# A derivative stored in the forward or recomputed in the backward: four layers of attention, forward and gradient, on one core

## The chip, the core and the metric

The kernel runs on one core of a Trainium2 chip. The core has five engines with their own instruction queues: PE (matrix products into PSUM, with weight loads beside them), DVE (elementwise and reductions), ACT (activations, copies), POOL (elementwise within SBUF) and SP (which here only issues transfers). ACT issues transfers too, from the same queue as its arithmetic. Every engine runs its queue in order. The metric is the time of one launch in microseconds; lower is better. "Granted clock" is the share of full speed that PE's clock had.

## The reference

Four layers over 2048 tokens of width 640, in 32 heads of 20, each with a normalisation in front and a residual around it: linear attention (A), sliding attention with a window of 256 (B), A, B. Both A layers share weights, as both B layers do.

```python
phi = lambda t: jnp.where(t > 0, t + 1, jnp.exp(t)) + 1e-6
pq, pk = phi(q), phi(k)
kv = jnp.einsum("bhsd,bhse->bhde", pk, v)
z = jnp.einsum("bhsd->bhd", pk)
num = jnp.einsum("bhqd,bhde->bhqe", pq, kv)
den = jnp.einsum("bhqd,bhd->bhq", pq, z)[..., None] + 1e-6
o = num / den
```

That is layer A, whose feature map is `phi`. Layer B is softmax attention. Outputs are the last x, the gradient for x and those for the four weight matrices; everything is bfloat16.

The derivative of `phi` is 1 for t > 0 and exp(t) otherwise, that is min(exp(t), 1). The kernel computes phi(t) as max(t, 1e-6) + min(exp(t), 1), so min(exp(t), 1) stands in a tile of its own on the way. From phi alone it can be had as min(phi - 1e-6, 1).

## The kernel before

Tokens are worked on in 16 tiles of 128. The layers are numbered 0 to 3 (A, B, A, B). The stages, with their places in the profiled span:

- First pass (up to about 120 us): for each tile normalise x (`ln`), multiply by layer 0's q, k and v weights, and apply `phi` (`a_qkv`, L488 to L538). Per half of 320 columns: PE into PSUM, ACT's exponential into a tile `ee` (L516), DVE's min with 1 in place (L517), DVE's max and add (L520) into `pp` (for q) or `gcar` (for k). `ee` is a ring of 4 buffers, `pp` one of 2. ACT copies part of v (L501). Results go to DRAM by transfers that ACT issues: `pq`, `pk`, `v`, and the two derivatives `eq` and `ek`.
- Token sums (`a_kv`): the products of pk and v, and pk's own sum, over all tokens. Three of five bands and the sum gather in the bank `pv_ps` (L597, L605) as the tiles come; these are fillers, which the order puts where PE has nothing else. The two other bands (`band_sum`, L579) take buffers of the ring `mm`, two PSUM banks that nearly all products share. DVE masks the sums into `mbd` and `zsel`.
- Joint passes, 0 and 2 (about 120 to 400 and 430 to 730 us; `ab_pass`): layers l and l+1 together, in a software pipeline over tiles. Steps of one tile are `num` (A's numerator and denominator, `a_num`, L448 and L646), `out` (A's projection, then layer l+1's normalisation), `qkv` (B's projections), the scores and weighted values of B's eight groups of heads (`attn`, L826, L830, L864), and `outb` (B's projection). Pass 0 has `a_first` for layer 2 behind that, k and v alone. Pass 2 has `late_q` for layer 2's q, and the first steps of the backward.
- Between the passes layer 2's sums are made; the first six tiles of its q (`EARLY`) are fillers there (`late_q`, matmuls L553, exponential L557); the weights are turned (L913), fillers too. The q of the first two tiles is turned by PE through a buffer of `mm` (L464), that of others by a transposing transfer on SP.
- Backward of layer 3 (about 740 to 1060 us), a stage for layers 3 and 2 (to 1460), backward of layer 1 (to 1770), a stage for layers 1 and 0 (to the end). In those two stages `lin_grads` (about 1220 to 1370, and 1940 to 2070 us) loads per tile pk, v and the numerator's gradient by transposing transfers, and the derivatives `eq` and `ek` by plain ones, all on SP. PE makes the gradients of phi(q) and phi(k) in PSUM, and DVE multiplies them by the derivative into `dqkv` (L1503). Beside it runs `tail`: PE's product with the weights, ACT's copy `dh` (L1309), DVE's `scr` (L1317), ACT's `w` (L1324), POOL's `gw` (L1327), DVE's update of `gcar` (L1329). In the stage for layers 3 and 2 also `local_dO`: PE's product, DVE's `slab` (L1370), POOL's `prod` (L1377), DVE's reduction (L1380) and two small ones (L1382, L1384), and a transfer `dOpt` that ACT issues.

Each engine's order in the forward and in the two stages is made ahead by a planner (`Sched.order`) from estimated costs: among the operations whose inputs it takes to be ready it picks the earliest start, then the place in the program (`prio`). Fillers are handicapped by 300 ns. A ring hands out its buffers in the program's order, so an operation that needs the ring's next buffer stands behind the one that is named earlier. In the forward PE's other operations may go at most `AHEAD` places past the first that isn't done. The program's order in a joint pass is sorted by positions: tile number plus an offset of each step, in the table `AT`, where 1.0 is one tile.

Of the kernel before, what the change touches and what calls it, by code (L numbers as in the profile page):

```python
# [20 lines left out]
LN_EPS = 1e-5  # L21
AHEAD = 19
IDLE = 300
# [179 lines left out]
class Kern:  # L203
    def __init__(self, ctx, tc, x0, A_wqkv, A_wo, B_wqkv, B_wo, grad_out, outs):
# [68 lines left out]
        for l in (0, 2):  # L273
            self.sv[l] = dict(
                pq=d.tile([T, D], BF, name=f"pq{l}"), pk=d.tile([T, D], BF, name=f"pk{l}"),
                eq=d.tile([T, D], BF, name=f"eq{l}"), ek=d.tile([T, D], BF, name=f"ek{l}"),
                v=d.tile([T, D], BF, name=f"v{l}"), o=d.tile([T, D], BF, name=f"o{l}"),
                r32=d.tile([T, self.H], F32, name=f"r32{l}"),
                mbd=d.tile([D, D + P], BF, name=f"mbd{l}"),
            )  # L280
# [53 lines left out]
    def forward(self, slabs):  # L334
# [5 lines left out]
        with ExitStack() as st:  # L340
# [72 lines left out]
            def dma(eng, out, in_, size, r, w, **kw):  # L413
                def f():
                    with nc.allow_non_contiguous_dma(reason="strided layouts"):
                        dq[eng].dma_start(out=out(), in_=in_())
                op(eng, 60, f, r, w, dma=("D", size), **kw)
# [70 lines left out]
            def a_qkv(l, tt, hnT):  # L488
# [3 lines left out]
                def chunk(ci):  # L492
                    def f():
# [29 lines left out]
                        if ci == 3 and "q" in c:  # L523
                            p_, e = c["p"], c["q"]
                            turn("s", lambda: pqT[:, :, tt * P:(tt + 1) * P], lambda: p_.t, DT, [(p_, 0), (p_, 1)],
                                 [("pqT", tt)])
                            dma("ACT", lambda: self.tm_view(sv["pq"])[:, tt, :], lambda: p_.t, 160 * KB,
                                [(p_, 0), (p_, 1)], [])
                            dma("ACT", lambda e=e: self.tm_view(sv["eq"])[:, tt, :], lambda e=e: e.t, 160 * KB,
                                [(e, 0), (e, 1)], [])  # L530
                        if ci == 3:
                            e = c["k"]
                            dma("ACT", lambda: self.tm_view(sv["pk"])[:, tt, :], lambda: pk[:, tt, :], 160 * KB,
                                [("pk", tt, 2), ("pk", tt, 3)], [])
                            dma("ACT", lambda e=e: self.tm_view(sv["ek"])[:, tt, :], lambda e=e: e.t, 160 * KB,
                                [(e, 2), (e, 3)], [])
                    return f
# [4 lines left out]
            def late_q(l, tt, where="s1", **F):  # L542
# [25 lines left out]
                dma("ACT", lambda: self.tm_view(sv["pq"])[:, tt, :], lambda: p_.t, 160 * KB, [(p_, 0), (p_, 1)], [], **F)  # L568
                dma("ACT", lambda: self.tm_view(sv["eq"])[:, tt, :], lambda: e.t, 160 * KB, [(e, 0), (e, 1)], [], **F)

# [392 lines left out]
            def a_first(items, l, base, lag=0.0, late=()):  # L963


                for tt in range(TT):
# [12 lines left out]

            EARLY = 6  # L980
            AT = {0: dict(num=-2.458, out=-1.707, outb=1.792, step=0.144, qkv=-0.99, wide=0.745, lag=0.42, af=2.042, al=-0.11),
                  2: dict(lq=-3.207, num=-2.403, out=-1.76, outb=1.696, step=0.086, qkv=-0.985, wide=0.584, lag=0.35, gT=0.745, dO=1.691, dOs=0.137)}

# [85 lines left out]
            a_kv(0)  # L1069
            ab_pass(0, False)  # L1070
            for tt in range(EARLY):
                late_q(2, tt, filler=True)
            a_kv(2)
            kv_users = {o for t in range(TT) for k in [("pk", t, 2), ("pk", t, 3), ("vv", t, 4), ("vv", t, 5)]
# [16 lines left out]
    def bwd_phase(self, lb, la, nb, ahead, raw):  # L1091
# [9 lines left out]
        with ExitStack() as st:  # L1101
# [363 lines left out]
            def lin_grads(tt, items, t0):  # L1465
# [4 lines left out]
                def start():  # L1470
                    for nm, src, size in (("dNT", self.tmp_dN, 192 * KB), ("pkT", sv["pk"], 160 * KB),
# [3 lines left out]
                             [("dNd", tt)] if nm == "dNT" else [], [b])  # L1475
                    c["eq"], c["ek"] = load("eq", sv["eq"], tt), load("ek", sv["ek"], tt)

# [415 lines left out]
```

## Time and profile before

| | |
|---|---|
| median of 3 runs | 2144.93 us (2142.76 to 2145.81) |
| the profiled execution | 2145.22 us, its span 2143.5 us |
| granted clock, mean | 0.975 |
| PE busy | 2008.2 us (94%) |
| DVE, ACT, POOL busy | 1440.1, 1203.3, 879.4 us |
| transfers | 376.43 MB, mean 176 GB/s |

The page names an instruction by its line and engine, then the tile written and those read. A time behind `<-` in brackets is what the engine idled before it and what ended the idling. `mm_ps`, `s_ps`, `pv_ps` and `dw_ps` are banks of PSUM. Tiles laid into the region `slabR` go by that name: there `slabR` can be the normalised rows, or in `lin_grads` the buffer of `ek`.

### The profile page before, as it was taken

How to read it: one execution, taken by the hardware profiler on the slowest of the kernel's cores; microseconds unless marked ns; L12 is line 12 of the kernel's file. 1: busy time of each engine (PE TensorE's matmuls, PEld its weight loads, DVE VectorE, ACT ScalarE, POOL GpSimd, SP SyncE). 2: the span in 40 equal slices, each digit the busy share in tenths (PEclk: the TensorE clock that was granted, in tenths of full speed). 3: DMA queues.
4: the chain of work that ended last, by engine and by line, in shares of the span. 5: the costliest groups of instructions: out<-in, count | busy, mean ns of one | idle time of the engine just before them, and what ended most of it. 6: DMA issues, size and time to landing. Idle time of an engine off the chain costs nothing. (4 is left out here: it accounts for less than half of the span.)

```text
span 2143.5 us, 68024 instructions
## 1 busy us (share of the span) xinstructions
PE 2008.2 (94%) x27908; PEld 1389.2 (65%) x27908; DVE 1440.1 (67%) x2954; ACT 1203.3 (56%) x1995; POOL 879.4 (41%) x1850
## 2 busy tenths in 40 slices
PE   6879999889999899999899999999999999999999
PEld 4656666656666577777666667656777765666764
DVE  6757777567776599999634368606998984444651
ACT  3527878647888589899422233216988881221430
POOL 1015666316777456666223223204665652230210
PEclk9989999999999899999899999999999999999999
DMA  9928989469998788987987899847999998989943
GB/s 291 256 106 179 191 193 191 119 198 201 210 208 191 146 157 151 161 161 155 193 185 168 213 200 203 175 104 142 157 158 151 170 170 162 199 185 227 186 111 102
DMA packets 943687, 376.43 MB, mean 176 GB/s; under 512 B 821776, under 2 KB 923664, under 8 KB 943120
## 3 DMA queue, kind: packets, MB, share of 16 engines
q1 hardware_dynamic: 866176, 299.16, 71.9%
q10 hardware_dynamic: 77200, 72.94, 11.1%
q8 instruction: 218, 3.57, 0.7%
q14 instruction: 93, 0.76, 0.1%
HBM read 109.02 MB, written 112.07 MB: 103 GB/s over the span
## 5 line engine op out<-in xcount | busy, mean ns | idle before, releaser
L1693 DVE TENSOR_TENSOR ds_sb<-pair,e_sb 128x768 bf16<-128x768 f32 x480 | 437.6, 951 | 57.8 <-PE pair L1654 49.6
L1673 ACT ACTIVATE e_sb<-pair 128x768 bf16<-128x768 f32 x480 | 390.9, 815 | 95.6 <-PE pair L1654 67.4
L839 POOL TENSOR_SCALAR_AFFINE_SELECT e_sb<-e_sb 128x384 bf16<-128x384 bf16 (+1 forms) x512 | 198.3, 406 | 357.5 <-ACT e_sb L830 335.7
L830 ACT ACTIVATE e_sb<-s_ps 128x1152 bf16<-128x1152 f32 (+2 forms) x256 | 273.8, 1070 | 100.2 <-PE s_ps L826 78.4
L1685 POOL TENSOR_SCALAR_AFFINE_SELECT e_sb<-e_sb 128x256 bf16<-128x256 bf16 x448 | 182.0, 406 | 227.1 <-ACT e_sb L1673 226.9
L1327 POOL TENSOR_TENSOR gw<-w,gcar 128x640 f32<-128x640 f32 x64 | 89.4, 1397 | 423.4 <-ACT w L1324 406.8
L1138 PEld LDWEIGHTS <-slabR 128*128 128x128 bf16 x1920 | 185.6, 98 | 116.1 <-DMA slabR<-o 3.7
L1682 POOL TENSOR_SCALAR_AFFINE_SELECT e_sb<-e_sb 128x256 bf16<-128x256 bf16 x512 | 206.5, 406 | 89.3 <-ACT e_sb L1673 89.3
L1718 PEld LDWEIGHTS <-dsT 128*128 128x128 bf16 x2880 | 146.2, 97 | 97.7 <-issue 91.5
L1709 ACT COPY dsT<-dsT_ps 128x768 bf16<-128x768 bf16 x240 | 191.2, 796 | 9.4 <-PE dsT_ps L1706 6.6
L448 PE MATMUL mm_ps<-slabR,hnTB 128*128 128x320 bf16 x960 | 170.5, 308 | 10.5 <-DVE gcar L520 6.0
L1706 PE MATMUL dsT_ps<-ident,ds_sb 128*128 128x128 bf16 x1848 | 158.2, 223 | 1.3 <-ACT dsT L1709 1.1
L1722 PEld LDWEIGHTS <-ds_sb 128*128 128x128 bf16 x2880 | 145.1, 96 | 0.8 <-issue 0.8
L1722 PEld LDWEIGHTS <-e_sb 128*128 128x128 bf16 x2880 | 145.0, 96 | 0.0
L844 POOL TENSOR_SCALAR_AFFINE_SELECT e_sb<-e_sb 128x512 bf16<-128x512 bf16 x224 | 142.6, 636 | 0.0
L833 ACT ACTIVATE e_sb<-s_ps 128x384 bf16<-128x384 f32 (+2 forms) x256 | 119.9, 468 | 32.3 <-PE s_ps L826 15.1
L1138 PE MATMUL dw_ps<-dqkv,slabR 128*128 128x480 bf16 x640 | 134.7, 366 | 0.0
L1309 ACT ACTIVATE dh<-mm_ps 128x320 f32<-128x320 f32 x64 | 28.0, 437 | 189.8 <-PE mm_ps L1138 164.9
L1138 PE MATMUL dw_ps<-dqkv,om 128*128 128x480 bf16 x640 | 134.2, 366 | 0.0
L1654 PE MATMUL pair<-slabR 32*128 32x384 bf16 (+2 forms) x1024 | 120.5, 326 | 12.0 <-DVE ds_sb L1693 5.2
L1138 PEld LDWEIGHTS <-om 128*128 128x128 bf16 x800 | 77.5, 98 | 71.3 <-DMA om<-o 2.4
L864 PEld LDWEIGHTS <-e_sb 128*128 128x128 bf16 x2880 | 105.5, 96 | 26.6 <-POOL e_sb L844 7.5
(234 smaller groups left out, 4357.6 us busy)
## 6 DMA issues: line engine op xcount, KB each, us to landing
qkvp<-qk_slab SPq DMA_DIRECT2D x64, 256.0 KB, 3.7
hn<-slabR SPq DMA_DIRECT2D x64, 160.0 KB, 2.9
qkvp<-v_slab SPq DMA_DIRECT2D x32, 256.0 KB, 3.4
slabR<-qkvp SPq DMA_DIRECT2D x16, 512.0 KB, 4.8
o<-o SPq DMA_DIRECT2D x48, 160.0 KB, 2.9
eq<-ee ACTq DMA_DIRECT2D x32, 160.0 KB, 3.0
pq<-pp ACTq DMA_DIRECT2D x32, 160.0 KB, 2.4
ek<-ee ACTq DMA_DIRECT2D x32, 160.0 KB, 2.7
```

Of the source, the lines that this page charges most:

```text
L448: nc.tensor.matmul(ps.t[:, w0:w0 + width], lhsT=lhsT(), rhs=rhs(), start=start, stop=stop)
L830: op("ACT", av(3 * nkt * P), lambda: nc.scalar.activation(e.t[:, 0:3, 0:nkt, :], s3.t[:, :, 0:nkt * P].rearrange("p h (i q) -> p h i q", q=P),
L839: nc.gpsimd.affine_select(out=v, in_=v, compare_op=ALU.is_ge, fill=0.0, base=0, pattern=[[0, h1 - h0], [1, P]], channel_multiplier=-1)
L1138: nc.tensor.matmul(ps.t[:, w0:w0 + width], lhsT=lhsT(), rhs=rhs(), start=start, stop=stop)
L1673: nc.scalar.activation(E[n][:, 2 * p:2 * p + 2], PR[h][:, :, 0:3 * P].rearrange("p i (j q) -> p i j q", q=P), ACT.Exp, scale=self.c_att)
L1682: nc.gpsimd.affine_select(out=e[:, :, j, :], in_=e[:, :, j, :], compare_op=ALU.is_ge, fill=0.0, base=0, pattern=[[0, 2], [-1, P]], channel ...
L1685: nc.gpsimd.affine_select(out=e[:, :, j, :], in_=e[:, :, j, :], compare_op=ALU.is_ge, fill=0.0, base=-1, pattern=[[0, 2], [1, P]], channel ...
L1693: nc.vector.tensor_mul(DS[n][:, hs], PR.pop(h)[:, :, 0:3 * P].rearrange("p i (j q) -> p i j q", q=P), E[n][:, hs])
L1706: nc.tensor.transpose(ps[:, i, j, :], DS[n][:, 2 * p + i, j, :], self.ident)
L1709: (nc.scalar.copy if by == "A" else nc.vector.tensor_copy)(TSB[h], TPS.pop(h))
L1718: nc.tensor.matmul(a[:, 0, hh, :], lhsT=TSB[2 * n + hh // 2][:, hh % 2, j, :], rhs=ld[g]["K"][:, k, cs], start=(i == 0), stop=(i == len(dq ...
L1722: nc.tensor.matmul(a[:, 1 + x, hh, :], lhsT=src[n][:, hh, j, :], rhs=ld[g][rhs][:, q, cs], start=(i == 0), stop=(i == len(dkv) - 1))
```

## The change

In the forward the derivatives `eq` and `ek` are no longer written to DRAM; their four DRAM tensors go, and with them 64 transfers of 160 KB that ACT issued. In `lin_grads` the buffers `eq` and `ek` are loaded from `pq` and `pk` instead, and DVE turns each into the derivative in place, min(phi - 1e-6, 1), with one instruction on 128x640. The multiplications are as before.

Between the passes the operations of `a_kv(2)` are set up ahead of the q fillers, so that they come first in the program's order and in the ring `mm`. `EARLY` is 8 instead of 6, `AHEAD` 17 instead of 19, and both rows of `AT` have new offsets.

```diff
-AHEAD = 19
+AHEAD = 17
...
-                eq=d.tile([T, D], BF, name=f"eq{l}"), ek=d.tile([T, D], BF, name=f"ek{l}"),
...
                         if ci == 3 and "q" in c:
...
-                            dma("ACT", lambda e=e: self.tm_view(sv["eq"])[:, tt, :], lambda e=e: e.t, 160 * KB,
-                                [(e, 0), (e, 1)], [])
                         if ci == 3:
...
-                            dma("ACT", lambda e=e: self.tm_view(sv["ek"])[:, tt, :], lambda e=e: e.t, 160 * KB,
-                                [(e, 2), (e, 3)], [])
...
             def late_q(l, tt, where="s1", **F):
...
-                dma("ACT", lambda: self.tm_view(sv["eq"])[:, tt, :], lambda: e.t, 160 * KB, [(e, 0), (e, 1)], [], **F)
...
-            EARLY = 6
-            AT = {0: dict(num=-2.458, out=-1.707, outb=1.792, step=0.144, qkv=-0.99, wide=0.745, lag=0.42, af=2.042, al=-0.11),
-                  2: dict(lq=-3.207, num=-2.403, out=-1.76, outb=1.696, step=0.086, qkv=-0.985, wide=0.584, lag=0.35, gT=0.745, dO=1.691, dOs=0.137)}
+            EARLY = 8
+            AT = {0: dict(num=-2.329, out=-1.53, outb=1.773, step=0.003, qkv=-0.851, wide=0.713, lag=0.391, af=2.216, al=-0.231),
+                  2: dict(lq=-3.14, num=-2.341, out=-1.768, outb=1.691, step=0.084, qkv=-0.988, wide=0.634, lag=0.313, gT=0.715, dO=1.598, dOs=0.307)}
...
             ab_pass(0, False)
+            a_kv(2)
             for tt in range(EARLY):
                 late_q(2, tt, filler=True)
-            a_kv(2)
...
-                    c["eq"], c["ek"] = load("eq", sv["eq"], tt), load("ek", sv["ek"], tt)
+                    for nm, p_ in (("eq", "pq"), ("ek", "pk")):
+                        c[nm] = b = load(nm, sv[p_], tt)
+                        op("DVE", 310, lambda b=b: nc.vector.tensor_scalar(
+                            out=b.t, in0=b.t, scalar1=-1e-6, scalar2=1.0, op0=ALU.add, op1=ALU.min), [], [b])
```

More of the change, by code (lines that the diff above doesn't have):

```diff
@@ L523, in f @@
                         if ci == 3 and "q" in c:
-                            p_, e = c["p"], c["q"]
+                            p_ = c["p"]
                             turn("s", lambda: pqT[:, :, tt * P:(tt + 1) * P], lambda: p_.t, DT, [(p_, 0), (p_, 1)],
@@ L528, in f @@
                                 [(p_, 0), (p_, 1)], [])
-                            dma("ACT", lambda e=e: self.tm_view(sv["eq"])[:, tt, :], lambda e=e: e.t, 160 * KB,
-                                [(e, 0), (e, 1)], [])
                         if ci == 3:
-                            e = c["k"]
                             dma("ACT", lambda: self.tm_view(sv["pk"])[:, tt, :], lambda: pk[:, tt, :], 160 * KB,
                                 [("pk", tt, 2), ("pk", tt, 3)], [])
-                            dma("ACT", lambda e=e: self.tm_view(sv["ek"])[:, tt, :], lambda e=e: e.t, 160 * KB,
-                                [(e, 2), (e, 3)], [])
                     return f
```

## The prediction

> **What bounds the kernel now.** I read the page's head first, then busy time by stretches cut where the work changes, then in each stretch that the change touches the waits, and last the order of instructions there.
>
> ```profile
> span 2143.5 us, 68024 instructions
> PE 2008.2 (94%) x27908; PEld 1389.2 (65%) x27908; DVE 1440.1 (67%) x2954; ACT 1203.3 (56%) x1995; POOL 879.4 (41%) x1850
> ```
> ```profile
> 20.00:110.00 90.00, 76.41 (x661) 55.10 (x662) 61.26 (x175) 49.95 (x124) 0.00 (x0) 0.95 0.96 257
> 165.00:400.00 235.00, 219.38 (x3817) 153.33 (x3814) 172.61 (x434) 190.56 (x313) 153.88 (x339) 1.00 0.86 185
> 400.00:485.00 85.00, 71.80 (x837) 51.24 (x835) 53.78 (x141) 36.66 (x78) 14.33 (x36) 0.90 0.55 162
> 485.00:720.00 235.00, 225.95 (x3887) 159.47 (x3885) 170.48 (x412) 185.88 (x278) 174.75 (x359) 1.00 0.96 200
> 1258.00:1362.00 104.00, 97.95 (x903) 74.49 (x901) 91.53 (x194) 33.09 (x86) 34.50 (x26) 1.00 0.98 197
> 1975.00:2065.00 90.00, 90.00 (x912) 71.04 (x910) 60.94 (x145) 37.05 (x96) 18.17 (x13) 1.00 0.83 173
> ```
>
> In the stretch rows the columns are length, then busy time of PE, weight loads, DVE, ACT, POOL, then granted clock, DMA share, GB/s. PE is busy 94% of the span, so only its idle time can be won. It idles 13.6 us in the first pass (20 to 110), 15.6 and 9.0 us in the two joint passes (165 to 400, 485 to 720), and 13.2 us between those (400 to 485), where the clock drops to 0.90 too. The two backward stretches at the end are where the derivative is used. They differ: at 1975 PE never idles and DVE is busy 61 of 90 us; at 1258 DVE is busy 91.5 of 104 us, 88%, beside a PE with 6.0 us idle. An added DVE instruction costs nothing in the one and may set the pace in the other.
>
> **The change part by part. 1: the stored derivatives leave the forward.** 64 writes of 160 KB go, all issued by ACT: 32 eq, 32 ek.
>
> ```profile
> PE s_ps L464 <- DVE slabR L482: 7.7, 3, 3.7
> PE s_ps L448 <- ACT vv L501: 4.4, 7, 1.1
> PE s_ps L464 <- ACT ee L516: 3.7, 6, 1.0
> ```
> ```profile
> L416 ACTq DMA_DIRECT2D eq<-ee x14: 326/333/989, 29.2 to 109.8; - x14
> ```
> ```profile
> 68.45 0.99 ACTq L416 DMA_DIRECT2D eq<-ee  x1
> 69.54 0.39 ACTq L416 DMA_DIRECT2D ek<-ee  x1
> 69.97 0.42 ACT L501 CAST vv<-s_ps 128x320 bf16<-128x320 f32 x1 [0.83 <-PE mm_ps L448]
> ```
> ```profile
> 70.44 0.84 PE L448 MATMUL s_ps<-Wqkv_A,hnTA 128*128 128x320 bf16 x5 [0.68 <-ACT vv L501]
> ```
>
> The first fence is PE's waits from 20 to 110 (total, times, longest). Here an issue costs more than its 0.33 us: at 68.45 ACT issues eq, then ek until 69.93, only then copies v's bank at 69.97, and PE, which needs that bank, stands 0.68 us. PE waits on ACT's v copy and exponentials total 4.4 + 3.7 = 8.1 us; a tile loses at least 2 x 0.33 = 0.66 us of ACT's issue (eq's shortest and median: 326, 333 ns). Gain: at least 0, at most the 8.1. I take 6, some 0.4 us in each of 15 tiles; DVE, busy 61 of 90 us, is late next, and the 7.7 us behind the normalised rows stays. In the joint passes ACT is busy 190.6 and 185.9 of 235 us, with 16 such issues in each (16 x 0.33 = 5.3 us of its queue):
>
> ```profile
> PE s_ps L826 <- ACT e_sb L830: 6.8, 13, 1.3
> ...
> PE mm_ps L464 <- DVE slabR L482: 4.9, 5, 2.6
> ```
> Of PE's waits from 165 to 720, that on the attention's exponentials (the first row) bounds what can come of it, 0 to 6.8 us; I take 1.5. The bytes themselves are hidden: none of PE's waits from 20 to 110 is for a transfer. Should the engines' orders, planned anew without these writes, come out worse, that is in part 3's bounds.
>
> **2: the sums set up ahead of q's fillers, eight q tiles instead of six.** Between the passes PE's order is now:
>
> ```profile
> 421.39 0.89 ACT L516 ACTIVATE ee<-mm_ps 128x320 bf16<-128x320 f32 x2 [2.70 <-DMA pk<-gcar]
> 422.18 0.43 ACT L557 ACTIVATE ee<-s_ps 128x320 bf16<-128x320 f32 x1
> ```
> ```profile
> 431.33 0.65 PE L464 MATMUL mm_ps<-ident,pp 128*128 128x128 bf16 x5
> 431.82 2.11 PE L579 MATMUL mm_ps<-vv,gcar 128*128 128x140 bf16 x32
> 433.77 0.28 PE L448 MATMUL mm_ps<-mbd,pqT 128*128 128x32 bf16 x5
> ...
> 470.59 0.71 PE L464 MATMUL mm_ps<-ident,slabR 128*128 128x128 bf16 x5 [2.57 <-DVE slabR L482]
> ```
>
> q's first two tiles are turned in the `mm` ring (the second at 431.33); the two last band sums (431.82, 2.11 us) stand behind them in that ring, and the next pass's first numerator (433.77) behind those. With the sums set up first they take the ring's buffers ahead of the turns, and fill the time in which q waits: its exponential can't run before k's last (422.18 behind 421.39, one ring). So the numerator needs only the second turn, 2.1 us earlier. I take 1.8, most of it; zero, if q's fillers, now outranked by the sums, come later by as much. The two further q tiles are 20 matmuls of 320 columns, 4 x 0.84 = 3.4 us by the five at 70.44: work taken out of a pass where PE is 96% busy and laid where it still stands 2.57 us at once (470.59). I take 1.7 of it. Together 3.5, from 0 to 8.3: of the 13.2 us idle there, 4.9 are the waits for the normalised rows (470.59 and four more), which the change leaves. Two more pq writes and two transposes go through ACT's and SP's queues there instead of later; none of PE's waits from 400 to 485 is for one.
>
> **3: new positions, a reach of 17 instead of 19.** No work is added or removed; each pass keeps its chain. The reach holds PE to fewer operations ahead, the steps of 0.003 put two chunks back to back. What the order costs now is PE's idle time in the passes, 15.6 + 9.0 us, of which part 1 took 1.5; a few of these can close or as many open. I take 0 and keep -6 to +6, a quarter of them either way.
>
> **4: DVE recomputes the derivative.** Loads stay as many, as large and on SP. Added are 2 instructions a tile, 32 in each backward stage, in place on 128x640.
>
> ```profile
> L482 DVE TENSOR_SCALAR slabR<-x,mv,rs x64: 430/446/774, 9.3 to 678.6; 128x640 bf16<-128x640 bf16 x64
> ```
> The same operation at the same size is 0.446 (0.430 to 0.774). I take 0.44, so 0.88 us a tile. The Trainium skill (Advanced Engine Details and Errata, VectorE Performance Modes) lets a bf16 tensor-scalar within SBUF run at four elements a cycle; by it an instruction would be some 0.3 us, an estimate, and the sum 3 us lower at most. The 0.446 row is of that kind and slower.
>
> In the last stage (1975) PE is full and DVE idle 29 of 90 us, 1.8 a tile: 0, or at worst 1 where a load lands late. In the first (1258) this is one tile:
>
> ```profile
> 1276.29 1.95 DVE L1329 SCALAR_TENSOR_TENSOR gcar<-slabR,sm,gw 128x640 bf16<-128x640 bf16 x1 [0.35 <-POOL gw L1327]
> ...
> 1284.87 1.95 DVE L1329 SCALAR_TENSOR_TENSOR gcar<-slabR,sm,gw 128x640 bf16<-128x640 bf16 x1 [0.35 <-POOL gw L1327]
> ```
> ```profile
> 1280.41 0.34 ACTq L1128 DMA_DIRECT2D dOpt<-slab  x1
> 1280.79 0.44 ACT L1309 ACTIVATE dh<-dw_ps 128x320 f32<-128x320 f32 x1 [2.08 <-PE dmB_ps L1167]
> ```
> ```profile
> DVE scr L1317 <- ACT dh L1309: 5.1, 10, 1.2
> DVE gcar L1329 <- POOL gw L1327: 5.0, 13, 0.7
> ```
>
> It is a ring of waits: ACT's queue holds dOpt's issue (1280.41) till DVE ends the slab, dh stands behind that (1280.79), DVE's scr waits for dh, gcar comes behind scr, and the next slab behind gcar. The period is 8.58 us here (1276.29 to 1284.87), and DVE stands only 5.1 + 5.0 us in all 13 tiles, 0.8 each. What falls into these waits is free; what falls elsewhere lengthens the ring by its length. Both ends: 0, and 16 x 0.88 = 14. The loads' places say where the added instructions go:
>
> ```profile
> 1276.12 0.38 SPq L1128 DMA_DIRECT2D eq<-eq  x1
> ```
> ```profile
> 1281.14 0.63 SPq L1128 DMA_DIRECT2D slabR<-ek  x1
> ```
> ```profile
> eq<-eq SPq DMA_DIRECT2D x32, 160.0 KB, 3.4
> ```
> With 3.4 us to land, eq is there at 1279.5, before dOpt's issue lets dh go: +0.44. ek is there at 1284.6, at gcar's wait (0.35 up to 1284.87): about 0. That is 13 x 0.44 = 5.7; I take 5. Behind a load that is late stand the products and the slab on DVE, and PE waits for them.
>
> **The sum.** -6 - 1.5 - 3.5 + 0 + 5 + 0 = -6. The profiled execution took 2145.2 us, 0.3 above the median 2144.9 of the runs shown: 2145.2 - 6 = 2139.2, or 2139.
>
> **The rivals.** *A, the added work is hidden.* The gcar instruction takes 1.95 us where POOL's prod runs beside it, and 0.87 where nothing does:
>
> ```profile
> 1276.22 1.34 POOL L1377 TENSOR_TENSOR prod<-slab,o 128x640 f32<-128x640 bf16 x1
> ```
> ```profile
> 1990.26 0.87 DVE L1329 SCALAR_TENSOR_TENSOR gcar<-hn,sm,gw 128x640 bf16<-128x640 bf16 x1
> ```
> An instruction put before gcar delays only its start, and it stands till prod ends anyway: 1.08 us a tile can take in the 0.88. Then the backward costs 0 and the time is 2134; a position gain of 3 makes it 2131. Against it: eq lands after gcar. The Trainium skill (SBUF — State Buffer, Who interferes with whom) has Vector and GpSimd share a port pair under an exclusive lock; the 1.95 beside 0.87 agrees. By the same rule a tensor-scalar can be shut out by gw or prod for up to an instruction of POOL's, which speaks against this change.
>
> *B, slower: the ring takes both instructions in full,* 16 x 0.88 = 14 us from 1240 on, and POOL keeps one of them standing, as it does gcar for 1.08 us, for a third as long in half the tiles, 8 x 0.36 = 3 us: 2145.2 - 11 + 17 = 2151, or 2154 where it does so in all. It decides from 11 us on, where the forward's gain is gone. For it: DVE is 88% busy, with 0.8 us of waiting in a tile. Against it: ek lands at one of those waits.
>
> *C, the forward gains nothing:* ACT's issues only hide DVE's pace in the first pass, and the fillers come later by what the sums come earlier. Then 2145.2 + 5 = 2150.
>
> **How the numbers follow.** Forecast 0.42, its own range 2133 to 2144; A 0.21; B 0.25; C 0.12. A measurement tells 0.2% from no change, 4.3 us about 2144.9. Faster: 0.32 of the forecast and all of A, 0.53. Within: 0.10 of the forecast, 0.05 of B, 0.04 of C, 0.19. Slower: 0.28. The range 2127 to 2155 takes in A with the positions' gain and B's end; the ends of all parts at once, 2116 (-8.1 - 6.8 - 8.3 - 6) and 2172 (+6 + 14 + 6 + 1), would need every unknown on one side.
>
> **What would show it.** In the first pass the 14 issues of pq take less than eq's 80.6 us (29.2 to 109.8) by some 6, and PE's 8.1 us on ACT shrink below 3. The first numerator comes some 2 us sooner behind the last v chunk. At 1258 the period of gcar rises from 8.6 us to 9.0, DVE over 90% busy; A shows 8.6 and a gcar under 1.95, B 9.5. At 1975 PE stays full. The forecast is wrong if a pass of 235 us moves by more than 6 us, or a DVE wait on the derivative's load appears.

## The result, and the profile after

The changed kernel takes 2127.86 us (median of 4 runs, 2125.01 to 2130.59); the kernel before took 2143.85 beside it (4 runs, 2141.27 to 2145.81). The ratio is 0.993, with a 95% interval from 0.9917 to 0.9944: faster by 16 us, where 6 were forecast. The profiled execution took 2125.0 us, 20.2 less than that of before (2145.2).

The head of the page and the busy time by stretches of the changed kernel (columns as in the prediction; the stretches are cut at about the same work as those of before, so all but the first begin 7 to 24 us earlier):

```profile
span 2123.3 us, 67887 instructions
PE 2004.6 (94%) x27908; PEld 1384.9 (65%) x27908; DVE 1457.3 (69%) x3018; ACT 1205.1 (57%) x1995; POOL 878.9 (41%) x1850
```
```profile
20.00:99.00 79.00, 75.07 (x675) 55.02 (x676) 60.42 (x177) 53.43 (x128) 0.00 (x0) 0.97 0.96 236
158.00:381.00 223.00, 215.74 (x3717) 150.06 (x3713) 173.75 (x425) 183.64 (x302) 149.10 (x329) 0.99 0.87 182
381.00:461.00 80.00, 68.96 (x849) 50.82 (x849) 54.23 (x146) 38.60 (x82) 14.55 (x36) 0.98 0.55 159
461.00:696.00 235.00, 226.17 (x3908) 157.78 (x3907) 166.25 (x406) 185.51 (x276) 175.45 (x361) 1.00 0.92 191
1235.00:1339.00 104.00, 100.33 (x914) 75.40 (x912) 97.18 (x219) 33.68 (x87) 34.96 (x26) 1.00 1.00 200
1954.00:2044.00 90.00, 88.78 (x892) 69.89 (x890) 67.85 (x168) 36.41 (x94) 18.17 (x13) 1.00 0.79 170
```

PE idles 3.9 us in the first pass (79.00 - 75.07) where it idled 13.6, and 7.3 in the first joint pass where it idled 15.6. Between the passes it idles 11.0 instead of 13.2, in the second joint pass 8.8 instead of 9.0. In the first backward stretch DVE went up from 91.5 to 97.2 of 104 us, and PE's idle time fell all the same, from 6.0 to 3.7.

For the comparison of all kernels I cut the span at instructions that every one of them has: the first copy of the sums into `zcol` ends the first pass, the last write of `oB` the first joint pass, and layer 3's backward begins with its first product `pair`; the two `lin_grads` columns run from the first to the last of `tail`'s products with `wq`, the loop that runs beside `lin_grads`. The experiments go by the numbers in their names (there is none numbered 4). The stages are those of one profiled execution each. The kernel before was run beside each group, with a median of 2141.95 us beside 1, 2, 5 and 6, 2142.91 beside 3, 7, 8 and 9, and 2143.08 beside 10 to 13; the ratios go by these. In us:

| kernel | first pass | first joint pass | up to the backward | first lin_grads | last lin_grads | median, ratio to before |
|---|---|---|---|---|---|---|
| before | 119.3 | 290.6 | 325.4 | 128.1 | 102.6 | 2143.85 |
| after | 108.4 | 281.8 | 321.2 | 127.1 | 103.7 | 2127.86, 0.993 (0.9917 to 0.9944) |
| 1 derivative alone | 109.2 | 301.5 | 321.5 | 127.5 | 103.1 | 2145.41, 1.0018 (1.0006 to 1.003) |
| 2 order alone | 120.0 | 286.6 | 328.4 | 126.2 | 102.8 | 2149.54, 1.0042 (1.0029 to 1.0055) |
| 3 after, old positions | 109.1 | 304.5 | 322.2 | 126.0 | 103.4 | 2147.22, 1.0018 (1.0006 to 1.0031) |
| 5 writes back on ACT | 120.0 | 286.0 | 328.0 | 126.9 | 103.4 | 2149.02, 1.0029 (1.0013 to 1.0046) |
| 6 writes back on SP | 116.6 | 282.1 | 326.4 | 127.0 | 103.1 | 2146.41, 1.0022 (1.0011 to 1.0033) |
| 7 after, reach 19 | 107.0 | 283.4 | 322.4 | 127.4 | 104.0 | 2129.53, 0.9934 (0.9915 to 0.9952) |
| 8 after, sums last | 108.0 | 283.5 | 320.0 | 127.2 | 103.1 | 2126.26, 0.992 (0.9902 to 0.9938) |
| 9 other bytes on SP | 117.0 | 284.1 | 319.6 | 126.7 | 103.6 | 2137.2, 0.9973 (0.9958 to 0.9987) |
| 10 derivative alone, o on SP | 108.7 | 291.0 | 322.6 | 127.6 | 103.7 | 2132.5, 0.9951 (0.9935 to 0.9966) |
| 11 after, two more DVE instructions | 108.5 | 283.3 | 320.5 | 143.4 | 105.8 | 2147.42, 1.0017 (1.0005 to 1.003) |
| 12 after, o on SP | 108.5 | 282.4 | 321.3 | 126.8 | 105.0 | 2134.01, 0.9951 (0.9932 to 0.9969) |
| 13 small writes on ACT | 117.1 | 283.9 | 329.2 | 126.4 | 104.0 | 2143.35, 1.0001 (0.9985 to 1.0018) |

From before to after that is -10.9 in the first pass, -8.8 in the first joint pass, -4.2 up to the backward, -1.0 and +1.1 in the two `lin_grads`; what is left of the -20.2, +3.6, lies in stretches whose code wasn't touched. Such stretches differ that much from one execution to the next (last section), so the medians carry the verdict and the stages the reasons.

### The profile page after: what moved, and what is told of

It is laid out like the page before. It is cut to its first block, busy times and chain, and to the rows that moved or that the text cites. A ratio compares the mean times of both kernels' runs of the same rounds, so it can differ in the third digit from the quotient of the medians.

```text
span 2123.3 us, 67887 instructions
## 1 busy us (share of the span) xinstructions
PE 2004.6 (94%) x27908; PEld 1384.9 (65%) x27908; DVE 1457.3 (69%) x3018; ACT 1205.1 (57%) x1995; POOL 878.9 (41%) x1850
## 5 line engine op out<-in xcount | busy, mean ns | idle before, releaser
L1650 PE MATMUL pair<-slabR 32*128 32x384 bf16 (+2 forms) x1024 | 121.4, 328 | 11.8 <-DVE ds_sb L1689 5.0
L857 PEld LDWEIGHTS <-e_sb 128*128 128x128 bf16 x2880 | 108.4, 96 | 31.8 <-POOL e_sb L837 8.1
L857 PE MATMUL pv_ps<-v_slab,e_sb 128*128 128x32 bf16 x2880 | 121.3, 177 | 5.4 <-POOL e_sb L837 4.5
L826 ACT ACTIVATE e_sb<-s_ps 128x384 bf16<-128x384 f32 (+2 forms) x256 | 119.3, 466 | 8.9 <-PE mm_ps L447 4.2
```

Of the source, the lines that this page charges most:

```text
L857: nc.tensor.matmul(pv.t[:, h % 16, :], lhsT=e.t[:, hh, j, :], rhs=vts[j].t[:, h, :], start=(j == 0), stop=(j == nkt - 1))
```

## The first pass: fewer bytes, fewer issues, or another order

The prediction put this gain on the issues of `eq` and `ek` in ACT's queue. PE's waits from 20 to 110 us in the changed kernel, and the issues of `pq` in the same time:

```profile
PE s_ps L463 <- DVE slabR L481: 4.0, 2, 3.9
...
PE s_ps L447 <- ACT vv L500: 1.6, 2, 1.4
```
```profile
L415 ACTq DMA_DIRECT2D pq<-pp x15: 332/333/381, 28.8 to 103.5; - x15
```

The waits for ACT went from 8.1 us to 1.6. But the wait for the normalised rows, which the prediction said would stay, went too, from 7.7 to 4.0. And a tile takes (103.5 - 28.8) / 14 = 5.34 us where it took 80.6 / 13 = 6.20: 0.86 less, more than the two issues' 0.66.

**Experiment 1, the derivative alone** (the writes gone and DVE recomputing, with the old positions, the old order of the sums, `EARLY` 6 and a reach of 19):

```diff
-AHEAD = 17
+AHEAD = 19
...
-            EARLY = 8
-            AT = (the new offsets)
+            EARLY = 6
+            AT = (the old offsets)
...
-            a_kv(2)
             for tt in range(EARLY):
                 late_q(2, tt, filler=True)
+            a_kv(2)
```

> The kernel before with the derivative's part of the change alone: no eq and ek writes in the forward, DVE's recomputation in the backward; positions, reach, EARLY and the order of the token sums as before. Theory W (the writes' issues in ACT's queue held the forward back): most of the change's 16 us comes here, 2130 to 2134, with the first pass ending near 108.4 us (zcol's first copy) instead of 119.3 and PE's wait on DVE's gcar in the first joint pass (6.0 us) gone. Theory P (the new positions made the gain): the first pass still ends near 108.4, since no position acts in it, but the first joint pass keeps its 6.0 us and the time is 2136 to 2139.

**Experiment 2, the order alone** (the other half: before, with those four edits the other way round):

> The kernel before with the order's part alone: AHEAD 17, EARLY 8, both rows of AT new, token sums of layer 2 set up ahead of q's fillers; eq and ek written and loaded as before. Theory W: within 4 us of the kernel before, first pass unchanged (zcol at 119.3). Theory P: 2132 to 2138, with the first joint pass some 10 us shorter and the first pass unchanged.

Each half alone is slower than before, by 3.5 and 7.6 us (before: 2141.95), and both together are 16 faster. Neither theory gave these times. The first pass belongs to the derivative's half, as both said: 109.2 in the one, 120.0 in the other. PE's wait for `gcar` in the first joint pass did go with the writes (6.0 us before, 0.2 in experiment 1), and the pass grew all the same. What the two halves do to each other is in the next section.

**Experiments 5 and 6, the writes put back into the changed kernel, on ACT or on SP.** Nothing reads them; this is data written in addition.

```diff
                             dma("ACT", lambda: self.tm_view(sv["pq"])[:, tt, :], lambda: p_.t, 160 * KB,
                                 [(p_, 0), (p_, 1)], [])
+                            dma("ACT" or "SP", lambda e=e: self.tm_view(sv["eq"])[:, tt, :], lambda e=e: e.t, 160 * KB,
+                                [(e, 0), (e, 1)], [])
... (ek behind pk, and eq in late_q, the same way)
```

> The changed kernel with the 64 writes of eq and ek put back on ACT's queue, read by nobody; the backward recomputes from pq and pk as in the changed kernel. Theory W: slower than the changed kernel by 10 to 16 us (2138 to 2144), the first pass ending near 119. Theory P: slower by 5 to 8 us only, all in the first pass. It differs from the order's part alone by DVE's recomputation, so the two together price that: within 2 us of it if the recomputation is hidden, 5 to 14 us above it if the ring of waits takes it.

> The same with the 64 writes issued by SP. If the writes cost by their issue in ACT's queue, this is the changed kernel's 2128 within 3 us, with the first pass ending near 108. If they cost by the transfers themselves (bandwidth, or ee's buffers held until a write lands), it is as slow as with the writes on ACT, 2138 to 2144.

With the writes on ACT the first pass is back at 120.0. On SP, without any issue in ACT's queue, it is still 116.6. So the issues on ACT are not needed for most of the loss. Both kernels (2149.0 and 2146.4) are slower than any theory had them. And experiment 5 is experiment 2 with the recompute added: 2149.0 beside 2149.5 us, so the recompute costs nothing that shows, the outcome that its expectation called hidden. PE's waits from 20 to 110 us with the writes on SP:

```profile
PE s_ps L464 <- DVE slabR L482: 6.4, 3, 3.9
PE s_ps L448 <- ACT vv L501: 5.4, 10, 0.8
```

PE waits for ACT's copy of v for 5.4 us although ACT issues nothing more than in the changed kernel: a wait for ACT doesn't mean that issues delay it.

**Experiment 9, the bytes without a hold on the exponential's ring** (48 writes of 160 KB on SP, with pk's tile as their source, so that no buffer of `ee` is kept; nothing reads them):

```diff
+                            for nm in ("eq", "ek")[l // 2:]:
+                                dma("SP", lambda nm=nm: self.tm_view(sv[nm])[:, tt, :], lambda: pk[:, tt, :], 160 * KB,
+                                    [("pk", tt, 2), ("pk", tt, 3)], [])
```

> The changed kernel with 48 extra writes of 160 KB on SP (two a tile in the first pass, one a tile for layer 2's k), taken from phi of k, which stays in place, so that no buffer of ee waits for a write to land; nobody reads them. With the derivatives written by SP from ee the first pass ended at 116.6 us, without writes at 108.4. If the held buffers cost it, the first pass ends at 108 to 110 here; if the transfers do, at 114 to 117.

117.0: the hold on `ee` isn't needed either. That left the bytes, with the transfer engines 0.95 to 1.00 busy from 20 to 110 us in before, 5, 6 and 9.

**Experiment 13, writes of 8 KB.** As experiment 5, with the same order of instructions on PE, DVE and ACT, but each write takes 32 columns instead of 640; the size that the planner is told is left at 160 KB.

```diff
-                            dma("ACT", lambda e=e: self.tm_view(sv["eq"])[:, tt, :], lambda e=e: e.t, 160 * KB,
+                            dma("ACT", lambda e=e: self.tm_view(sv["eq"])[:, tt, 0:32], lambda e=e: e.t[:, 0:32], 160 * KB,
...
```

> The changed kernel with the derivative's writes put back on ACT, which nothing reads, as in the fifth experiment and with the same order of instructions on PE, DVE and ACT, but each writes 32 columns (8 KB) instead of 640 (160 KB). Theory I (my prediction: the issues in ACT's queue are what the first pass pays for, the bytes are hidden): the first pass still ends at 117 to 120 us (the fifth: 120.0, the changed kernel 108.4) and the kernel stays at 2145 to 2149. Theory J (the bytes: the DMA engines are full there): the first pass ends at 108 to 113 us; ACT's issues alone are worth 0 to 4.

The theory of bytes failed. First the stretch from 20 to 110 us in the changed kernel, then in this one, then PE's waits in this one:

```profile
20.00:110.00 90.00, 84.32 (x779) 62.26 (x780) 67.01 (x200) 57.10 (x135) 0.00 (x0) 0.97 0.87 218
```
```profile
20.00:110.00 90.00, 77.71 (x681) 56.74 (x682) 62.24 (x178) 51.80 (x128) 0.00 (x0) 0.95 0.86 211
```
```profile
PE s_ps L464 <- DVE slabR L482: 8.4, 3, 3.9
PE s_ps L448 <- ACT vv L501: 3.3, 6, 1.1
PE s_ps L464 <- ACT ee L516: 3.0, 6, 0.9
```

The transfers are as light as in the changed kernel (0.86 and 211 GB/s beside 0.87 and 218), and the first pass still ends at 117.1. Against experiment 5, whose order is the same, the bytes are worth 120.0 - 117.1 = 2.9 us (2.2 against before). The other 8.7 to the changed kernel's 108.4 are not bytes, and experiment 6 loses 8.2 without those issues on ACT. (The whole kernel, at 2143.35, is some 2 us faster than theory I had it.)

What all the slow first passes have in common is that PE is told to work in another order than in the changed kernel. The planner books each transfer on one channel (`chan = max(chan, t) + size / 300`), so a planned write moves what it takes to be ready, and every engine's order is written anew, whichever engine issues the write. PE's instructions in program order, at the start of the first pass; T is the turning of a tile's normalised rows, Q that of q's features, h a product of 320 columns, s a group of token sums:

```
after, 1, 3, 7, 8, 10 to 12   T hhhh T h Q hhh T hhh Q hhh T hhh s Q hhh T hhh s Q hhh T hhh s Q hhh T hhh s Q hhh
6                             T hhhh T h Q hhh T hh Q hhhh T hh Q hhhh T hh s Q hhhhh s T h Q hhhhh s s T h Q hhhh
before, 2, 5, 13              T hhhh T h Q hhh T hh Q hhhh T hh Q hhhhh s s T h Q hhhhh s s h T h Q hhh T hh Q hhhh
```

The kernels of the first line have one and the same order on PE throughout the first pass, and end it at 107.0 to 109.2; those of the last line have another one in common, and end it at 119.3 to 120.0 with the full writes and at 117.1 with the small. Experiment 9 is like 6 in kind. Without the planned writes each tile goes the same way, three chunks, the turn, three chunks. With them the turn of q's features comes a chunk earlier, and in places (`Q hhhhh s s T`) five chunks and the sums stand ahead of the next turn of rows. At the first such place in experiment 13 PE stands 3.58 us for `slabR`. (Of the 8.4 us above, 3.94 fall at 20.3 us, where the changed kernel stands 3.88 as well.)

That wait has a second cause, which the rows of ACT and then of PE show:

```profile
40.84 0.44 ACT L516 ACTIVATE ee<-s_ps 128x320 bf16<-128x320 f32 x1 [2.08 <-DMA slabR<-in_B_wqkv_dram]
```
```profile
42.65 0.72 PE L464 MATMUL s_ps<-ident,slabR 128*128 128x128 bf16 x5 [3.58 <-DVE slabR L482]
```

ACT stood until the load of a weight had landed, which this exponential doesn't read, and DVE's normalised rows came behind the exponential. In front of it in ACT's queue was the issue of `v`, at 40.45. In these traces the issues of ACT and SP share eight semaphores (counters that tell of landings and on which engines wait), and no issue starts before the transfer ahead of it on the same semaphore has landed: `v` had that load ahead of it, issued by SP at 35.82 and landed at 40.36, and its own data since 38.76. So an issue can hold ACT for longer than it takes itself, and a transfer issued by SP can be what holds it. But the sum of such holds (those over 0.15 us, from 18 to 100 us) doesn't sort the kernels: ACT is held 2.7 us in experiment 6, 3.3 in before and 4.3 in 13, which are slow, and 3.7 in 8 and 4.6 in 3, which end the pass at 108.0 and 109.1. The order does sort them, and so does having more transfers to issue. What I hold for the cause of most of this gain is the order. Another order is what 5, 6, 9 and 13 have in common against the changed kernel, besides the added transfers. It is not isolated: a kernel with the new order and the writes issued without the planner's knowledge, and one with the old order and no writes, would have done that, and were not run. Until then it stays possible that issues alone, or bytes alone, each suffice to bring the pass to 117.

## The joint passes: the new positions need the writes gone, and the reverse

**Experiment 3, the changed kernel with the old positions** (only the table `AT` taken back):

> The changed kernel with both rows of AT as before (reach 17, EARLY 8, sums first and the recomputation stay). Without the writes the old positions gave a first joint pass, from zcol's first copy to the last oB, of 301.5 us, against 281.8 with all of the change. If the positions do that, this pass is near 300 us here and the time 2143 to 2150. If the reach of 17 does it, the pass is near 283 and the time 2128 to 2132.

With the old positions and without the writes the first joint pass takes 304.5 us (experiment 1: 301.5). With the writes and the old positions, which is before, 290.6. With the new positions it is 281.8 to 283.5 without the writes (the changed kernel, 7, 8, 11, 12) and 282.1 to 286.6 with them (2, 5, 6, 9, 13). Taking the writes away costs 11 us under the old positions (301.5 against 290.6) and gains up to 5 under the new. The new positions are worth 4 us with the writes (experiment 2) and 20 to 23 without (1, 3).

ACT's instructions in experiment 1 show where the 11 us come from (start, duration, engine; `ACTq` rows are issues of transfers), and PE's row behind them:

```profile
235.30 0.49 ACT L826 ACTIVATE e_sb<-s_ps 128x384 bf16<-128x384 f32 x1
235.98 0.38 ACTq L415 DMA_DIRECT2D pk<-gcar  x1
236.40 0.47 ACTq L415 DMA_DIRECT2D o<-oB  x1
236.91 1.54 ACTq L415 DMA_DIRECT2D linv<-slabR  x1
238.56 1.13 ACT L823 ACTIVATE e_sb<-s_ps 128x1152 bf16<-128x1152 f32 x1 [2.76 <-PE mm_ps L447]
```
```profile
239.74 0.35 PE L819 MATMUL s_ps<-QT,KT 32*128 32x128 bf16 x12 [1.68 <-ACT e_sb L823]
```

The three issues of a tile stand in a row from 235.98 to 238.45, right in front of an exponential whose scores have long been in PSUM (PE's last score row ahead of it starts at 235.82 and takes 0.35). PE stands 1.68 us for it. (The bracket at 238.56 names a product of PE that the exponential doesn't read; the issue ends 0.11 us ahead of it.) In before `ek`'s issue came behind `pk`'s, and the next exponentials ran before `o`'s and `linv`'s:

```profile
227.71 0.34 ACTq L416 DMA_DIRECT2D pk<-gcar  x1
228.09 0.45 ACTq L416 DMA_DIRECT2D ek<-ee  x1
228.59 0.49 ACT L833 ACTIVATE e_sb<-s_ps 128x384 bf16<-128x384 f32 x1 [1.05 <-PE s_ps L826]
228.80 0.33 ACTq L416 DMA_DIRECT2D o<-oB  x1
```

**Experiment 10 tests that:** experiment 1, with the attention's `o` and `linv` issued by SP.

```diff
-                            dma("ACT", lambda: self.tm_view(self.sv[l]["o"])[:, b, :], lambda: o.t, 160 * KB, ks, [])
-                            dma("ACT", lambda: self.tm_view(self.sv[l]["linv"])[:, b, :], lambda: lv.t, 16 * KB,
+                            dma("SP", lambda: self.tm_view(self.sv[l]["o"])[:, b, :], lambda: o.t, 160 * KB, ks, [])
+                            dma("SP", lambda: self.tm_view(self.sv[l]["linv"])[:, b, :], lambda: lv.t, 16 * KB,
```

> The first experiment (derivative recomputed, everything else as before the change, 2145.4 us), with one more edit: the attention's o and linv are written by SP instead of ACT, so that pk's, o's and linv's issues no longer stand in a row in ACT's queue before an exponential. From the end of the first pass to the last o of the first joint pass it took 301.5 us, against 290.6 before and 281.8 after the change. Theory Q (the old positions lose because, with ek's write gone, the three issues close up in front of an exponential and PE waits 1 to 2 us for it in each tile): that stage falls to 283 to 292 us and the kernel to 2128 to 2137. Theory R (the old positions are late for another reason, the row of issues only fills a hole): the stage stays at 298 or more and the kernel at 2142 or more.

The stage falls to 291.0 and the kernel to 2132.5: theory Q. PE's wait for these exponentials in the first joint pass, first in before (119 to 410 us), then in experiment 1 (109 to 411), in experiment 10 (109 to 400), and in the changed kernel (108 to 390), where the new positions lay the issues beside exponentials instead:

```profile
PE s_ps L826 <- ACT e_sb L830: 3.6, 8, 1.3
```
```profile
PE s_ps L819 <- ACT e_sb L823: 11.8, 14, 1.8
```
```profile
PE s_ps L819 <- ACT e_sb L823: 1.5, 3, 0.6
```
```profile
PE s_ps L819 <- ACT e_sb L823: 1.2, 3, 0.6
```

From 1 to 10 the wait lost 10.3 us and the stage 10.5. (The planner ordered the engines anew here too; but the one wait is as large as the loss.) From before to 1 it grew by 8.2 of the 11 us. The 9 us from 10 to the changed kernel's 281.8 are not taken apart.

**Experiment 12, the same edit in the changed kernel:**

> The changed kernel with the attention's o and linv written by SP instead of ACT. Theory Q (issues in ACT's queue ahead of exponentials are what the joint pass pays for): the new positions have them beside exponentials already, PE's wait on exponentials is only 1.2 us in the first joint pass, so 0 to 3 us faster than the changed kernel, 2124 to 2128. If SP's queue holds them behind waiting loads and the buffers of o are late: 2130 to 2136.

The first joint pass is 282.4, as without the edit: the 1.2 us of waiting left nothing to gain. The kernel is no faster (2134.0; 2128.3 to 2137.9), and its one profiled execution lost 8.8 us in layer 3's backward, at a lower clock (last section); whether the edit has to do with that is open. The time lies in the range that was given for `o` held up in SP's queue, but the joint passes show nothing of it (282.4 and 321.3 us).

**Experiments 7 and 8: the reach at 19, and the sums set up behind the fillers again.**

```diff
-AHEAD = 17
+AHEAD = 19
```

> The changed kernel with the reach at 19. If the reach matters, the first joint pass (281.8 us in the changed kernel) grows to 290 or more and the time is 2136 or more; if the positions alone do it, the pass stays within 3 us and the time within 2126 to 2131.

```diff
-            a_kv(2)
             for tt in range(EARLY):
                 late_q(2, tt, filler=True)
+            a_kv(2)
```

> The changed kernel with layer 2's token sums set up behind q's fillers again, EARLY still 8. By the prediction's second part the stretch from pass 0's last oB to the first pair of the backward (321.2 us in the changed kernel) grows by some 2 us and nothing ahead of it moves. The rival, that the place in the program hardly matters because q's exponential waits for k's in either, gives a change under 1 us.

Neither moves the time: 2129.5 and 2126.3, within the changed kernel's own 2125.0 to 2130.6. PE between the passes, in the changed kernel and then with the sums last:

```profile
402.20 1.52 PE L447 MATMUL mm_ps<-Wqkv_A,pqT 128*128 128x320 bf16 x10 [0.21 <-DVE gcar L519]
403.62 2.11 PE L572 MATMUL mm_ps<-vv,gcar 128*128 128x140 bf16 x32
...
411.53 0.44 PE L906 MATMUL s_ps<-ident,Wqkv_A 128*128 128x128 bf16 x5 [1.43 <-ACT KT L911]
...
413.76 0.44 PE L463 MATMUL mm_ps<-ident,pp 128*128 128x128 bf16 x5
414.04 0.28 PE L447 MATMUL mm_ps<-mbd,pqT 128*128 128x32 bf16 x5
```
```profile
403.60 1.52 PE L447 MATMUL mm_ps<-Wqkv_A,pqT 128*128 128x320 bf16 x10 [0.21 <-DVE gcar L519]
...
411.85 2.11 PE L572 MATMUL mm_ps<-vv,gcar 128*128 128x140 bf16 x32
413.80 0.28 PE L447 MATMUL mm_ps<-mbd,pqT 128*128 128x32 bf16 x5
```

The two band sums do come 8.2 us earlier (403.62, not 411.85). The next numerator doesn't: 414.04 - 402.20 = 11.8 us behind the last v chunks, against 413.80 - 403.60 = 10.2 with the sums last, and 433.77 - 422.69 = 11.1 before. It waits for the turn of q's second tile (413.76), and q's chunks wait in the `s_ps` banks behind the turned weights and ACT's copies of them (1.43 us at 411.53). The sums filled a hole that they had only to stand in.

## The backward: the recompute

The new instruction, and a tile of it in the first `lin_grads`; then DVE's waits from 1235 to 1339:

```profile
L1471 DVE TENSOR_SCALAR eq<-eq x32: 314/319/733, 1043.2 to 2036.7; 128x640 bf16<-128x640 bf16 x32
```
```profile
1254.94 1.95 DVE L1322 SCALAR_TENSOR_TENSOR gcar<-slabR,sm,gw 128x640 bf16<-128x640 bf16 x1 [0.35 <-POOL gw L1320]
1256.81 0.31 DVE L1471 TENSOR_SCALAR slabR<-slabR 128x640 bf16<-128x640 bf16 x1
...
1259.48 0.32 DVE L1471 TENSOR_SCALAR eq<-eq 128x640 bf16<-128x640 bf16 x1
1259.72 0.49 DVE L1164 COPY gT<-dmA_ps 128x640 bf16<-128x640 bf16 x1
1260.12 0.82 DVE L1310 CUSTOM_DVE_ANT_0 scr<-dh,slabR 128x640 bf16<-128x640 f32 x1
```
```profile
DVE gcar L1322 <- POOL gw L1320: 4.6, 12, 0.7
...
DVE scr L1310 <- ACT dh L1302: 0.4, 1, 0.4
```

An instruction is 0.32 us, not 0.44. It delays the next by 0.24 (1256.81 to 1257.05, 1259.48 to 1259.72), so a tile gets 0.48. `scr` now starts without a wait: it waited 5.1 us in 13 tiles before and waits 0.4 now, 0.36 a tile, and that took in most of the 0.48. `gcar` is still 1.95 beside POOL's `prod`.

**Experiment 11, the dose doubled:** behind each recompute a second instruction on the same tile that changes nothing (add 0, min with 1).

```diff
                         op("DVE", 310, lambda b=b: nc.vector.tensor_scalar(
                             out=b.t, in0=b.t, scalar1=-1e-6, scalar2=1.0, op0=ALU.add, op1=ALU.min), [], [b])
+                        op("DVE", 310, lambda b=b: nc.vector.tensor_scalar(
+                            out=b.t, in0=b.t, scalar1=0.0, scalar2=1.0, op0=ALU.add, op1=ALU.min), [], [b])
```

> The changed kernel with each of the recomputing DVE instructions followed by a second one that changes nothing (add 0, min with 1): 64 more of 0.32 us. If the first backward linear-gradient stage still has waiting to take them in (theory S, as for the first two instructions): that stage stays within 1.5 us of its 127.1 and the kernel within 2 us of the changed kernel. If the ring of waits is used up (theory T): 13 to 16 tiles times 0.32 to 0.64 us more, the stage at 131 to 137 and the kernel 4 to 10 us slower than the changed one. In the last stage, where PE is full, 0 to 2 us either way.

The first `lin_grads` takes 143.4 us, 16.3 more, beyond what either theory gave. The update of `gcar` in before, after and here (start of the first and the last of the 16):

```profile
L1329 DVE SCALAR_TENSOR_TENSOR gcar<-slabR,sm,gw x16: 885/1947/1951, 1253.5 to 1377.4; 128x640 bf16<-128x640 bf16 x16
```
```profile
L1322 DVE SCALAR_TENSOR_TENSOR gcar<-slabR,sm,gw x16: 883/1948/1965, 1231.8 to 1354.7; 128x640 bf16<-128x640 bf16 x16
```
```profile
L1322 DVE SCALAR_TENSOR_TENSOR gcar<-slabR,sm,gw x16: 873/882/1950, 1237.7 to 1377.1; 128x640 bf16<-128x640 bf16 x16
```

The period is 123.9 / 15 = 8.26 us before, 122.9 / 15 = 8.19 after, and 139.4 / 15 = 9.29 with the double dose. But the last of the 15 intervals is 15.5 us there, and 9.7 in the other two kernels. The 14 ahead of it take 8.85 us each, and 8.09 in the changed kernel: the first two instructions cost nothing, the next two 0.76 us a tile or 10.7 in all. Two things come together in that. The waiting in the ring is gone, so the full length counts. And `gcar` falls beside `prod` in 6 tiles where it did in 14, which gives back 8 x 1.07 = 8.6 us; the new instructions fall beside POOL's instead. DVE and POOL in experiment 11:

```profile
1277.58 1.38 DVE L1471 TENSOR_SCALAR eq<-eq 128x640 bf16<-128x640 bf16 x1
```
```profile
1277.38 1.40 POOL L1320 TENSOR_TENSOR gw<-w,gcar 128x640 f32<-128x640 f32 x1 [3.76 <-ACT w L1317]
```

An instruction of 0.32 us takes 1.38 where it begins beside POOL's `gw`, and ends 0.18 us after it (1278.96 and 1278.78); beside `prod` one takes 1.34. That happens to 13 of the 52 recorded from 1229 to 1373, which is 13 x 1.05 = 13.6 us on DVE. The lock on the shared port pair in the Trainium skill (SBUF — State Buffer, Who interferes with whom) agrees with these rows.

The other 5.8 us (15.5 against 9.7) are order again, in the last tile of experiment 11 (PE, then DVE):

```profile
1363.57 0.72 PE L1160 MATMUL dmA_ps<-ident,gcar 128*128 128x128 bf16 x5 [3.82 <-DVE gcar L1322]
```
```profile
1373.59 0.82 DVE L1310 CUSTOM_DVE_ANT_0 scr<-dh,slabR 128x640 bf16<-128x640 f32 x1 [8.42 <-ACT dh L1302]
```

There PE turns `gcar` ahead of the tile's products with `wq`, and `dh` and `scr` come late behind that; in the changed kernel the products come first (from 1342.98, the turn at 1350.30).

In the last `lin_grads` DVE now waits for its load of `ek` (from 1954 to 2044 us):

```profile
DVE ek L1471 <- DMA ek<-pk: 12.0, 11, 2.4
```

12 us of waiting, and the stage is 1.1 longer: DVE has the time there.

## Why the prediction was right or wrong

The sign, the size within the range, and the faster side were right. The sum came out at -6 where -16 were measured (-20.2 between the two profiled executions), and most of its terms were wrong singly. The measured 2127.9 is 0.9 us inside the lower end of the range, and outside the forecast's own 2133 to 2144: that it stayed within is luck.

- **1, the first pass, -6 (0 to -8.1): measured -10.9, and not by that mechanism alone.** The step that failed is "an issue costs more than its 0.33 us" as the whole account, with "the bytes themselves are hidden" beside it, and the planner's new order put aside as something that could only come out worse. Issues do cost more than 0.33 us, as `v`'s at 40.45 shows, but that doesn't sort the slow kernels from the fast. Bytes are worth 2.9 (5 against 13), and to look for transfers in PE's waits alone was too narrow: ACT's hold ended as one landed; with no such issue on ACT the pass still takes 116.6 (6). The order is what I hold to carry the rest; no run shows it by itself. What was to show this term right, `pq`'s issues some 6 us shorter, came out as 11 (13 x 0.86), and the 8.1 us fell below 3 as said. Both agreed with a mechanism that the runs don't bear out as the whole.
- **1, the joint passes, -1.5.** No single value is right for it: taking the writes away costs 11 us in the first joint pass under the old positions and gains 0 to 5 under the new. Up to the backward the kernels planned without these writes in the second pass take 319.6 to 322.6 us, those with them 325.4 to 329.2, so 4 of the gain lie there.
- **2, sums first and eight early tiles, -3.5: nothing from the sums.** 2126.3 without that edit, 2127.9 with it. The step that failed is that "the numerator needs only the second turn, 2.1 us earlier": the second turn itself was late, behind the turned weights. The numerator came 0.7 us later behind the last v chunk (11.8 against 11.1), not 2 sooner. `EARLY` by itself wasn't tried; experiments 1 and 3 differ in it (and in the sums and the reach), and reach the backward in 321.5 and 322.2 us.
- **3, new positions, 0 (-6 to +6): wrong in kind.** I took it as noise around a fixed chain. It is worth 4 us with the writes and 20 to 23 without, and in part because an issue's place in ACT's queue decides whether PE waits for an exponential (10.5 us, experiment 10). The reach is worth nothing (7).
- **4, the recompute, +5: measured -1.0 and +1.1.** Two steps failed: the duration (0.32, not 0.44: the row I took reads its two scalars from tiles, this one has them in the instruction. The estimate of 0.3 from the Trainium skill, Advanced Engine Details and Errata, VectorE Performance Modes, agrees), and the place: `eq`'s instruction ran right ahead of `gT` and `scr`, where DVE had stood for `dh`, not in the part of the ring that counts. Experiments 2 and 5 agree that it costs nothing (2149.5 and 2149.0). The period of 9.0 did not come; DVE went to 93%, as forecast. The last stage is slower by 1, the end that was kept for late loads, and the late loads are there; PE stands 1.2 of 90 us in it, where it was to stay full.
- **The rivals.** A had the outcome of the backward, hidden, by another mechanism: nothing of it in the 1.08 us of `gcar`, which stood as long as before, most of it in `scr`'s wait (0.36 of 0.48 us a tile). B is wrong at two instructions a tile, and right in its mechanism at four, POOL's hold included (10.7 us). C is out.
- **What would make it wrong** was named as a pass that moves by more than 6 us (the first joint pass moved by 8.8) and a wait on the derivative's load (12 us, in the last stage). Both came. The total stayed in the range because a gain that was too small, in the first passes, and a cost that didn't come, in the backward, lay on the same side, inside the allowance for position.

## What to carry to other kernels

Where a planner writes the order, an edit that only removes work still moves everything: read the order of both kernels first, and before giving the gain to issues or bytes, run one kernel that keeps the order. Two halves of a change can each lose and together win, so price them in a two-by-two and not as terms of a sum. For an instruction added to a busy engine count the waits that can take it in, and look for what runs beside its new place: the second dose cost 10.7 us in the ring, and 5.8 by another order, where the first cost none.

## What the runs showed of the hardware that I had not expected

Three issues in a row can hold ACT far longer than three times 0.33 us: 0.38, 0.47 and 1.54 us above, 2.5 in all, with the arithmetic behind them standing.

The same DVE operation on 128x640 in bf16 takes 0.446 us where its two scalars are read from tiles (the prediction's row) and 0.319 where they are numbers in the instruction; that this difference is the cause was not tried by itself.

Stretches with the same code differ between executions by more than most terms here. Layer 3's backward in experiment 10, and in experiment 12:

```profile
722.00:1039.00 317.00, 300.56 (x6289) 218.73 (x6288) 280.00 (x411) 272.03 (x361) 183.47 (x480) 0.97 0.88 159
```
```profile
712.00:1039.00 327.00, 306.06 (x6284) 220.56 (x6283) 280.75 (x410) 272.27 (x360) 183.50 (x480) 0.93 0.87 154
```

The work of every engine is the same to 2% and the granted clock is 0.97 and 0.93; the stretch is 10 us longer. What lowers the clock in one execution and not in the next was not found.
